# First and last batch: spectral products for f and S/2 - f stay apart, and the inverse transform sums them over five contraction tiles

## The chip, the cores and the metric

The kernel runs on one core of one Trainium2 chip. The metric is the device time of one execution in microseconds (us), lower is better; 215.07 is the median of three runs. A profiled execution is recorded beside them.

## What is computed

Per batch of 8: an attention that goes through 32 packed rows for each of 8 heads, then a gated long convolution over the sequence of S = 576.

```
p_packed = softmax(scale * p k^T) v
x        = softmax(scale * q p_packed^T) p_packed      # [8, 576, 512], heads side by side
x1, x2, x3 = split(x @ w_proj, 3)
x2_conv  = irfft(rfft(x2) * rfft(filter))              # along the sequence
out      = (x1 * x2_conv * x3) @ w_out
```

## The kernel before, in words

A batch goes through four stages. **front** loads kn, vn and qn (by GpSimd's DMA queue), transposes keys (kTp) and queries (qTp) on TensorE, forms both softmaxes (scores s1 and s2, exponentials e1 and e2 on ScalarE, values pv, sums zs, and the normalised weights a2 on GpSimd). **turn** projects (qp, copied by ScalarE to qm; `project(1, 0)` is one unit of four PSUM banks, `project(2)` one of two), transforms the attention weights along the sequence (fp, ez, fa) and transposes them (a2t). **middle** forms the spectrum in five tiles f0 to f4, multiplies it with the filter's spectrum (h3, htail) into tt and gm, and forms the gates x1 and x3 (their product w on VectorE). **back** does the inverse transform (x2), multiplies with w into y and yt, and projects out (o, os, written by the sync engine's queue). `together` interleaves the stages of neighbouring batches; batch 0's middle and back and batch 7's stand partly alone, at the two ends of the program.

The spectrum is folded. Frequencies f = 1 to 128 and S/2 - f share their cosine and sine rows up to a sign that depends on whether the time index is even or odd. In `spectrum(m)`, which runs in the order m = 0, 2, 1, 3, 4, tiles 0 and 2 belong to one half of the complex product and tiles 1 and 3 to the other: VectorE multiplies a tile with two filter rows (tt0 to tt3, 128 x 1024 in fp32), and GpSimd adds tt0 + tt2 and tt1 + tt3. After m = 3, four adds and subtractions of 128 x 512 combine those two sums into gm parts 0 and 1 (for even time columns) and 2 and 3 (for odd ones). gm part 4 is the tail tile. For batches 1 to 6 GpSimd does all four; for batches 0 and 7 VectorE does parts 0 and 1, and GpSimd 2 and 3.

`inverse(m)` then makes, for each 128 of the 512 channels, a block of 288 even and 224 odd time columns with three matmuls each (two gm parts of that parity and the tail; ac holds the three tables), and `inverse_left` the last 64 odd columns for all four channel blocks in one bank.

The order of the work on each engine is not that of the code. All operations are recorded, and a planner simulates the five engines and the DMA queues and lists the operations in the order in which it would start them: on every engine the earliest recorded operation that is ready and whose buffers are free (`fits`). PSUM has eight banks (tag "ps"), at most six for the kinds "attention" and "transform" each. A unit, such as a projection, starts only when all its banks are free at once. The planned order is fixed at build time, so an engine that waits blocks all that stands behind it in its queue. Line 344 (354 after the change) is the recorder's call and so the line of nearly every row.

Of the kernel before, what the change touches and what calls it, by code (L numbers as in the profile page):

```python
# [14 lines left out]
ALU = mybir.AluOpType  # L15
AX = mybir.AxisListType

P = 128
SC_Y = float(2.0 ** 16)
# [13 lines left out]
COLUMN_T = np.concatenate([TILE_T[1], TILE_T[3], TILE_T[4], TILE_T[2][:64], TILE_T[0], TILE_T[2][64:]])  # L33
# [4 lines left out]
def _f16(x):  # L38
    return np.asarray(x, dtype=np.float64).astype(np.float16)


def _constants(S):
    F = S // 2 + 1
    t = np.arange(S, dtype=np.float64)
    f = np.arange(F, dtype=np.float64)
    ang = 2.0 * np.pi * np.outer(f, t) / S
    wre = np.cos(ang)
    wim = -np.sin(ang)
    cf = np.full(F, 2.0)
# [12 lines left out]

    inv = np.stack([
        are[F_LO], aim[F_LO],
        np.concatenate([are[F_TAIL], are[0:1], -are[F_TAIL], are[F - 1:F],
                        aim[F_TAIL], zero, aim[F_TAIL], zero], axis=0)])


    wc = np.zeros((P, 4, 384), dtype=np.float16)
    wt = np.zeros((P, 2, 640), dtype=np.float16)  # L70
    for i in range(4):
        wc[:, i, 0:256] = _f16(low[:, TILE_T[i]].T)
        wc[:, i, 256:384] = _f16(tail[:, TILE_T[i]].T)
    wt[0:32, 0, 0:256] = _f16(low[:, TILE_T[4][0:32]].T)
    wt[32:64, 0, 256:512] = _f16(low[:, TILE_T[4][32:64]].T)
    wt[0:64, 0, 512:640] = _f16(tail[:, TILE_T[4]].T)
    wt[64:128, 1, :] = wt[0:64, 0, :]
    ac = _f16(inv[:, :, COLUMN_T].transpose(1, 0, 2))
    return wc, wt, np.ascontiguousarray(ac)


# [55 lines left out]
class Recorder:  # L137
# [62 lines left out]
    def plan(self):  # L200
# [56 lines left out]
            ops = op.unit or [op]  # L257
            return {r[0] for o in ops for r in o.writes + o.reads if r[0] in self.slot and r[0] not in opened}

        def fits(op):  # L260
            if op.unit and (op is not op.unit[0] or any(o.need != o.inner for o in op.unit)):
                return False
            more = {}
            for t in news(op):
                for tag, _ in self.slot[t]:
                    more[tag] = more.get(tag, 0) + 1
            if any(used[tag] + n > limit[tag] for tag, n in more.items()):
                return False
            return op.what != "dma_start" or op.engine != "POOL" or lanes[0] > 0

        def release(op, same):
            for o in op.then:
# [5 lines left out]
        def issue(e, t):  # L278
            while free[e] <= t + 1e-6:
                if e == "PE" and rest:  # L280
                    op = rest.pop(0)
                else:
                    op = min((o for o in ready[e] if fits(o)), key=lambda o: o.n, default=None)
                    if op is None:
                        return
                    for x in news(op):
                        opened.add(x)
                        for tag, _ in self.slot[x]:
                            used[tag] += 1
                    rest.extend((op.unit or [op])[1:])  # L290
                ready[e].remove(op)
                order.append(op)
                if op.what == "dma_start":
                    took = 760 if e == "POOL" else 60
                    if e == "POOL":
                        lanes[0] -= 1
                    at(t + took + (2000 if e == "POOL" else 1500), "start", op)
                else:
                    took, land = product(op, t) if e == "PE" else (op.ns(), op.ns() + 60)
                    at(t + land, "done", op)  # L300
                    release(op, True)
                free[e] = t + took
                at(t + took, "free", e)
# [47 lines left out]
def kernel(  # L351
# [16 lines left out]
    ND = DM // P  # L368
# [22 lines left out]
    def psm(name, shape, dtype=FP32):  # L391
        return nc.tile(ps, shape, dtype, "ps", 8, name, ("transform", 6))
# [326 lines left out]
    def middle(b):  # L719

        s = st[b]
        a2t, qm, fa = s["a2t"], s["qm"], s["fa"]
        gm = sb([P, 5, DM], FP16, tag="gm", name=f"gm_b{b}")
        w = sb([P, ND, S], FP32, tag="w", name=f"w_b{b}")
        s["gm"], s["w"] = gm, w
        tt = {}

        def spectrum(m):
            f = psm(f"f{m}_b{b}", [P, DM])
            for t in range(2):  # L730
                nc.tensor.matmul(f[:], fa[:, t, ts(m, P)], qm[:, t, ts(1, DM)], start=(t == 0), stop=(t == 1))
            if m == 4:
                nc.vector.tensor_tensor(out=gm[:, 4, :], in0=f[:], in1=htail[:], op=ALU.mult)
                return
            r = m % 2
            x = tt[m] = sb([P, 2, DM], FP32, tag=f"tt{m // 2}", name=f"tt{m // 2}_b{b}", bufs=2)
            h = h3[:, r, 1:3, :] if m == 0 or m == 3 else h3[:, r, 0:2, :]
            nc.vector.tensor_tensor(out=x[:], in0=f[:].unsqueeze(1).broadcast_to([P, 2, DM]), in1=h, op=ALU.mult)
            if m >= 2:
                nc.gpsimd.tensor_tensor(out=x[:], in0=tt[r][:], in1=x[:], op=ALU.add)  # L740
            if m == 3:
                g = [tt[2], tt[3]]
                even = nc.vector if b in (0, B - 1) else nc.gpsimd

                even.tensor_tensor(out=gm[:, 0, :], in0=g[0][:, 0, :], in1=g[1][:, 0, :], op=ALU.add)
                even.tensor_tensor(out=gm[:, 1, :], in0=g[0][:, 1, :], in1=g[1][:, 1, :], op=ALU.subtract)
                nc.gpsimd.tensor_tensor(out=gm[:, 2, :], in0=g[0][:, 0, :], in1=g[1][:, 0, :], op=ALU.subtract)
                nc.gpsimd.tensor_tensor(out=gm[:, 3, :], in0=g[0][:, 1, :], in1=g[1][:, 1, :], op=ALU.add)

        def gate(*ms):  # L750

            cols = slice(0, MAIN) if len(ms) == 1 else slice(MAIN, S)
            n = cols.stop - cols.start
            x1 = psm(f"x1_b{b}", [P, len(ms), n])
            x3 = psm(f"x3_b{b}", [P, len(ms), n])
            for x, c0 in ((x1, 0), (x3, 2 * DM)):
                for m in ms:
                    for t in range(2):
                        nc.tensor.matmul(x[:, m - ms[0], :], qm[:, t, ds(c0 + m * P, P)], a2t[:, t, cols],
                                         start=(t == 0), stop=(t == 1))  # L760
            x1s = sb([P, len(ms), n], FP32, tag="x1s", name=f"x1s_b{b}", bufs=2)
            nc.scalar.copy(out=x1s[:], in_=x1[:])
            nc.vector.tensor_tensor(out=w[:, ms[0]:ms[-1] + 1, cols], in0=x1s[:], in1=x3[:], op=ALU.mult)

        for n, m in enumerate((0, 2, 1, 3, 4)):
            spectrum(m)
            yield 1100
            if n < 4:
                gate(n)
                yield 870  # L770
        gate(*range(ND))
        yield 460
    pair = [None]

    def back(b):

# [5 lines left out]
            pair[0] = sb([P, ND, 2, 64], FP16, tag="yt", name=f"yt_b{b}", bufs=1)  # L782
        yt = pair[0]

        def inverse(m):
            x2 = psm(f"x2_b{b}", [P, MAIN])
            for e, cols in enumerate((slice(0, EVEN), slice(EVEN, MAIN))):
                for j in range(3):
                    nc.tensor.matmul(x2[:, cols], gm[:, 4 if j == 2 else 2 * e + j, ts(m, P)], ac[:, j, cols],
                                     start=(j == 0), stop=(j == 2))  # L790
            nc.vector.scalar_tensor_tensor(out=y[:, m, :], in0=w[:, m, 0:MAIN], scalar=SC_Y, in1=x2[:],
                                           op0=ALU.mult, op1=ALU.mult)

        def inverse_left():
            x2 = psm(f"x2t_b{b}", [P, ND, 64])
            for m in range(ND):
                for j in range(3):
                    nc.tensor.matmul(x2[:, m, :], gm[:, 4 if j == 2 else 2 + j, ts(m, P)], ac[:, j, MAIN:S],
                                     start=(j == 0), stop=(j == 2))
            nc.vector.scalar_tensor_tensor(out=yt[:, :, x, :], in0=w[:, :, MAIN:S], scalar=SC_Y, in1=x2[:],  # L800
                                           op0=ALU.mult, op1=ALU.mult)

        def project_out(n):

# [19 lines left out]
        for m in range(ND):  # L824
            inverse(m)
            yield 660
        inverse_left()
        yield 350
        for n in range(5 if x else 4):
            project_out(n)  # L830
# [71 lines left out]
```

## Time and profile before

| | |
|---|---|
| runs | 214.38, 215.07, 216.06 us; median 215.07 |
| profiled execution | 215.93 us, span 214.1 us from first to last instruction |
| mean granted TensorE clock | 0.953 |
| TensorE matmul busy | 187.0 us, 87% of the span |
| VectorE, ScalarE, GpSimd busy | 149.5, 127.4, 140.1 us |

Batches overlap, so these shares are means over stages with different limits. In a timeline row stand the start, the length, the engine, the operation with the tiles it writes and reads (buffer numbers left out, so x_b is any of x1, x2, x3), its shape, how often it was repeated, and in brackets the idle time before it with what ended it. A matmul's length includes its way through the array; the pace is read from the starts.

### The profile page before, as it was taken

To read this page: it belongs to the slowest core of one execution; us is meant where nothing else is said; L and a number is where in the kernel's file an instruction comes from. 1 tells how busy PE (TensorE), PEld (TensorE's weight loads), DVE (VectorE), ACT (ScalarE), POOL (GpSimd) and SP (SyncE) were. 2 spreads that over 40 slices of the span, in tenths; PEclk is the share of its full clock that TensorE was granted. 3 is DMA by queue.
4 is the path that set the end of the run, shared out by engine and by line. 5 is a ranking of instruction groups with operands and counts; after the bars stand their busy time and mean duration, and the time that the engine had idled before them with its cause. 6 is when DMAs were issued, how large, how long until landed. Compare 5 with 4: busy or idle time off the path is not lost.

```text
span 214.1 us, 5815 instructions
## 1 busy us (share of the span) xinstructions
PE 187.0 (87%) x2418; PEld 117.0 (55%) x2418; DVE 149.5 (70%) x276; ACT 127.4 (59%) x269; POOL 140.1 (65%) x112
## 2 busy tenths in 40 slices
PE   0777559994999999999999999999999999997890
PEld 0225427651866566566765676566756565653540
DVE  4243837999257959886796699477957987698530
ACT  2236567593187897785757766777687846334040
POOL 8612388659464769989966699179447995945500
PEclk9999958997699999999999999999999999999796
DMA  5999999999999999069489990043013103405016
GB/s 123 285 217 202 207 197 201 207 197 193 164 168 218 237 156 144 4 92 236 129 112 159 149 215 3 8 134 106 3 49 94 59 0 124 127 0 182 19 65 180
DMA packets 36523, 28.71 MB, mean 134 GB/s; under 512 B 8016, under 2 KB 31056, under 8 KB 36496
## 3 DMA queue, kind: packets, MB, share of 16 engines
q0 software_dynamic: 29312, 16.52, 57.0%
q1 hardware_dynamic: 6464, 11.10, 17.0%
q10 hardware_dynamic: 720, 0.72, 1.1%
q8 instruction: 19, 0.31, 0.6%
q14 instruction: 8, 0.07, 0.1%
HBM read 35.41 MB, written 9.44 MB: 209 GB/s over the span
## 4 chain that ended last, share of the span: by engine, by line
PE 65%; DVE 16%; DMA 6%; POOL 5%; issue 3%; ACT 2%; DVEq 0%; POOLq 0%
PE x_b L344 20%; PE o_b L344 13%; PE f_b L344 7%; DMA kn_b<-in_k_dram 6%; PE fp_b L344 6%; PE s_b L344 4%; DVE tt_b L344 3%; PE qTp_b L344 3%; DVE gm_b L344 3%; PE pv_b L344 2%; DVE zs_b L344 2%; PE kTp_b L344 2%; PE qp_b L344 2%; POOL gm_b L344 2%; PE a2tp_b L344 2%
## 5 line engine op out<-in xcount | busy, mean ns | idle before, releaser
L344 POOL TENSOR_TENSOR tt_b<-tt_b,tt_b 128x1024 f32<-128x1024 f32 x16 | 37.7, 2359 | 14.4 <-DVE tt_b L344 14.4
L344 DVE TENSOR_TENSOR tt_b<-f_b,h 128x1024 f32<-128x1024 f32 x32 | 38.9, 1218 | 6.4 <-PE f_b L344 4.4
L344 PE MATMUL x_b<-a2t_b,qm_b 128*128 128x512 f16 (+1 forms) x256 | 42.0, 286 | 0.4 <-DVE w_b L344 0.3
L344 POOL TENSOR_TENSOR gm_b<-tt_b,tt_b 128x512 f16<-128x512 f32 x28 | 36.6, 1337 | 0.5
L344 ACT ACTIVATE os_b<-o_b 128x512 f32<-128x512 f32 x36 | 21.5, 607 | 23.7 <-PE o_b L344 23.5
L344 PE MATMUL x_b<-ac,gm_b 128*128 128x288 f16 (+1 forms) x192 | 30.5, 295 | 5.0 <-DVE gm_b L344 4.7
L344 PE MATMUL o_b<-wout,y_b 128*128 128x512 f16 x128 | 33.6, 380 | 0.2 <-DVE y_b L344 0.2
L344 PEld LDWEIGHTS <-gm_b 128*128 128x128 f16 x288 | 22.9, 104 | 15.0 <-DVE gm_b L344 5.7
L344 ACT CAST qm_b<-qp_b 128x512 f16<-128x512 f32 x48 | 25.1, 609 | 4.7 <-PE qp_b L344 4.4
L344 POOL TENSOR_TENSOR fa_b<-ez_b 128x512 f16<-128x512 f32 x14 | 17.5, 1269 | 14.7 <-ACT ez_b L344 14.7
L344 ACT COPY x1s_b<-x_b 128x512 f32<-128x512 f32 (+1 forms) x40 | 22.3, 560 | 8.2 <-PE x_b L344 8.0
L344 DVE TENSOR_TENSOR w_b<-x1s_b,x_b 128x512 f32<-128x512 f32 (+1 forms) x40 | 24.9, 625 | 1.6 <-ACT x1s_b L344 1.4
L344 ACT ACTIVATE e_b<-s_b 96x384 f16<-96x384 f32 (+1 forms) x48 | 23.5, 532 | 3.8 <-PE s_b L344 3.7
L344 PE MATMUL f_b<-qm_b,fa_b 128*128 128x512 f16 x80 | 24.0, 380 | 0.0
L344 PEld LDWEIGHTS <-a_b 128*128 128x128 f16 x240 | 17.1, 101 | 11.6 <-POOL a_b L344 2.8
L344 DVE SCALAR_TENSOR_TENSOR y_b<-w_b,x_b 128x512 f16<-128x512 f32 x32 | 20.3, 678 | 3.2 <-PE x_b L344 3.1
L344 PEld LDWEIGHTS <-qm_b 128*128 128x128 f16 x256 | 15.9, 98 | 8.9 <-issue 1.6
L344 PEld LDWEIGHTS <-y_b 128*128 128x128 f16 x128 | 12.1, 98 | 12.2 <-DVE y_b L344 1.1
L344 POOL TENSOR_TENSOR a_b<-e_b,zr_b 128x1152 f16<-128x1152 f16 (+2 forms) x10 | 17.3, 1742 | 0.7 <-DVE zr_b L344 0.5
L344 ACT COPY ez_b<-fp_b 128x512 f32<-128x512 f32 x16 | 9.8, 610 | 12.2 <-PE fp_b L344 12.2
L344 PE MATMUL kTp_b<-ident,kn_b 96*128 96x96 f16 x192 | 12.4, 206 | 1.0 <-DMA kn_b<-in_k_dram 0.8
L344 PEld LDWEIGHTS <-kn_b 96*128 96x128 f16 x192 | 10.5, 97 | 3.9 <-DMA kn_b<-in_k_dram 1.3
(78 smaller groups left out, 300.6 us busy)
## 6 DMA issues: line engine op xcount, KB each, us to landing
out_dram<-os_b SPq DMA_DIRECT2D x24, 256.0 KB, 2.6
kn_b<-in_k_dram POOLq DMA_DIRECT2D x8, 576.0 KB, 11.4
vn_b<-in_v_dram POOLq DMA_DIRECT2D x8, 576.0 KB, 12.7
qn_b<-in_q_dram POOLq DMA_DIRECT2D x8, 512.0 KB, 9.1
out_dram<-os_b SPq DMA_DIRECT2D x16, 128.0 KB, 2.4
wp<-in_moe_w_proj_dram POOLq DMA_DIRECT2D x3, 512.0 KB, 20.7
filt<-in_moe_filter_fft_dram SPq DMA_DIRECT2D x4, 256.0 KB, 6.5
out_dram<-os_b SPq DMA_DIRECT2D x16, 64.0 KB, 2.1
```

The lines of the kernel that those rows point to most:

```text
L344: ins = op.call(*op.args, **op.kw).ins
```

## The change

For batches 0 and 7 (`APART`) the four combining adds after m = 3 are gone. GpSimd's two adds, in fp32 as before on their way in, write gm parts 0 and 1 (products for f, ready after m = 2) and 2 and 3 (products for S/2 - f, after m = 3) directly in fp16. The inverse transform of these batches sums five contraction tiles: parts 0 and 1 over all 512 columns in one matmul each, parts 2 and 3 with tables that differ between even and odd columns, so that each takes two matmuls (288 and 224 columns), and the tail over all 512. The last 64 columns take five matmuls per channel block in place of three. The table ac grows from three parts to four (576 KB in place of 432). For batches 1 to 6 the arithmetic is as it was, but all four combining operations stay on GpSimd as before.

The planner also changes for all batches: when a unit is ready and finds too few free banks, the banks that it wants are held back, so that no later recorded operation may open a new one ahead of it (`held`, `choose`).

```diff
-    ac = _f16(inv[:, :, COLUMN_T].transpose(1, 0, 2))
+    inv = inv[:, :, COLUMN_T]
+    ac = _f16(np.stack([*inv, np.where(COLUMN_T % 2 == 0, -inv[1], -inv[0])]).transpose(1, 0, 2))
...
-            if any(used[tag] + n > limit[tag] for tag, n in more.items()):
+            if any(used[tag] + held.get(tag, 0) + n > limit[tag] for tag, n in more.items()):
+                if op.unit:
+                    for tag, n in more.items():
+                        held[tag] = max(held.get(tag, 0), n)
                 return False
...
+        def choose(e):
+            held = {}
+            return next((o for o in sorted(ready[e], key=lambda o: o.n) if fits(o, held)), None)
...
-            if m >= 2:
+            if apart and m >= 2:
+                nc.gpsimd.tensor_tensor(out=gm[:, 2 * r:2 * r + 2, :], in0=tt[r][:], in1=x[:], op=ALU.add)
+            elif m >= 2:
                 nc.gpsimd.tensor_tensor(out=x[:], in0=tt[r][:], in1=x[:], op=ALU.add)
-            if m == 3:
+            if m == 3 and not apart:
                 g = [tt[2], tt[3]]
-                even = nc.vector if b in (0, B - 1) else nc.gpsimd
...
+        def terms(x2, m, cols):
+            both = slice(cols.start, min(cols.stop, EVEN)), slice(max(cols.start, EVEN), cols.stop)
+            if b in APART:
+                yield x2, gm[:, 0, ts(m, P)], ac[:, 0, cols]
+                yield x2, gm[:, 1, ts(m, P)], ac[:, 1, cols]
+                for j in (0, 1):
+                    for e, c in enumerate(both):
+                        if c.start < c.stop:
+                            yield (x2[:, c.start - cols.start:c.stop - cols.start], gm[:, 2 + j, ts(m, P)],
+                                   ac[:, j if e == j else 3, c])
+                yield x2, gm[:, 4, ts(m, P)], ac[:, 2, cols]
```

Three places show how the order of instructions moves. The first is TensorE at the start of batch 0's inverse transform. Before, it stood behind both projection units of batch 1 (qp) and all key transposes of batch 2, and its first matmul was one for 288 columns:

```order
L344 LDWEIGHTS ppk1_77
L344 MATMUL qp_b1_213<-wp_68,ppk1_77 32x512
L344 LDWEIGHTS ppk1_77
L344 MATMUL qp_b1_214<-wp_68,ppk1_77 32x512
L344 LDWEIGHTS gm_b0_162
L344 MATMUL x2_b0_209<-ac_67,gm_b0_162 128x288
L344 LDWEIGHTS gm_b0_162
L344 MATMUL x2_b0_220<-ac_67,gm_b0_162 128x288
```

Now two matmuls for 512 columns follow the last gate matmul (x3) of batch 0 at once, and the unit of four projection banks comes behind them:

```order
L354 MATMUL x3_b0_202<-a2t_b0_141,qm_b0_133 128x64
L354 LDWEIGHTS gm_b0_162
L354 MATMUL x2_b0_209<-ac_67,gm_b0_162 128x512
L354 LDWEIGHTS gm_b0_162
L354 MATMUL x2_b0_209<-ac_67,gm_b0_162 128x512
L354 LDWEIGHTS ppk1_77
L354 MATMUL qp_b1_211<-wp_68,ppk1_77 32x512
```

Behind that unit (16 matmuls) stand 12 key transposes, one more 512-column pass, and only then the first matmul with part 2. The other projection unit, the other 12 key transposes and 12 scores are now spread among the rest of the inverse.

The second place is GpSimd's queue around the two adds of batch 0 (tt or gm written from tt0 and tt1; a2 is batch 1's normalisation). Before:

```order
L344 TENSOR_TENSOR tt1_b0_174<-tt0_b0_165,tt1_b0_174 128x1024
L344 DMA kn_b3_204<-in_k_dram 96x8x384
L344 DMA vn_b3_205<-in_v_dram 96x8x384
L344 TENSOR_TENSOR tt1_b0_196<-tt0_b0_189,tt1_b0_196 128x1024
L344 TENSOR_TENSOR a2_b1_184<-e2_b1_183,zr_b1_186 128x1152
L344 TENSOR_TENSOR gm_b0_162<-tt1_b0_174,tt1_b0_196 128x512 x2
L344 DMA qn_b3_206<-in_q_dram 128x8x256
```

After:

```order
L354 DMA kn_b3_204<-in_k_dram 96x8x384
L354 TENSOR_TENSOR gm_b0_162<-tt0_b0_165,tt1_b0_174 128x1024
L354 DMA vn_b3_205<-in_v_dram 96x8x384
L354 DMA qn_b3_206<-in_q_dram 128x8x256
L354 TENSOR_TENSOR gm_b0_162<-tt0_b0_189,tt1_b0_196 128x1024
L354 TENSOR_TENSOR a2_b1_184<-e2_b1_183,zr_b1_186 128x1152
```

The issue of kn moved ahead of the first add and that of qn ahead of the second; the two combining adds are gone.

The third place is TensorE at the end, behind the last gate matmul of batch 7. Before, the first matmuls of all four channel blocks need a combined part:

```order
L344 MATMUL x3_b7_764<-a2t_b7_693,qm_b7_674 128x64
L344 LDWEIGHTS gm_b7_728
L344 MATMUL x2_b7_767<-ac_67,gm_b7_728 128x288
L344 LDWEIGHTS gm_b7_728
L344 MATMUL x2_b7_768<-ac_67,gm_b7_728 128x288
L344 LDWEIGHTS gm_b7_728
L344 MATMUL x2_b7_769<-ac_67,gm_b7_728 128x288
```

Now six passes over 512 columns, with parts 0 and 1 for three channel blocks, stand ahead of the first that needs part 2 or 3; here the last of the six and what follows:

```order
L354 MATMUL x2_b7_769<-ac_67,gm_b7_728 128x512
L354 LDWEIGHTS gm_b7_728
L354 MATMUL x2_b7_769<-ac_67,gm_b7_728 128x512
L354 LDWEIGHTS gm_b7_728
L354 MATMUL x2_b7_767<-ac_67,gm_b7_728 128x288
L354 LDWEIGHTS gm_b7_728
L354 MATMUL x2_b7_767<-ac_67,gm_b7_728 128x224
```

TensorE has 24 matmuls more in all, 12 for each of the two batches. In batches 1 to 6 the four-bank unit of `project(1, 0)` now comes ahead of `project(2)` and of some key transposes and gates, with its four casts on ScalarE; before it came behind them.

More of the change, by code (lines that the diff above doesn't have):

```diff
@@ L258, in news, with fits @@
             return {r[0] for o in ops for r in o.writes + o.reads if r[0] in self.slot and r[0] not in opened}
-        def fits(op):
+        def fits(op, held):
             if op.unit and (op is not op.unit[0] or any(o.need != o.inner for o in op.unit)):
@@ L282, in issue @@
                 else:
-                    op = min((o for o in ready[e] if fits(o)), key=lambda o: o.n, default=None)
+                    op = choose(e)
                     if op is None:
@@ L725, in middle @@
         s["gm"], s["w"] = gm, w
-        tt = {}
+        tt, apart = {}, b in APART
         def spectrum(m):
@@ L738, in spectrum @@
             nc.vector.tensor_tensor(out=x[:], in0=f[:].unsqueeze(1).broadcast_to([P, 2, DM]), in1=h, op=ALU.mult)
-            if m >= 2:
+            if apart and m >= 2:
+                nc.gpsimd.tensor_tensor(out=gm[:, 2 * r:2 * r + 2, :], in0=tt[r][:], in1=x[:], op=ALU.add)
+            elif m >= 2:
                 nc.gpsimd.tensor_tensor(out=x[:], in0=tt[r][:], in1=x[:], op=ALU.add)
-            if m == 3:
+            if m == 3 and not apart:
                 g = [tt[2], tt[3]]
-                even = nc.vector if b in (0, B - 1) else nc.gpsimd
[L745 to L748, printed above, removed]
+                for n, r, op in ((0, 0, ALU.add), (1, 1, ALU.subtract), (2, 0, ALU.subtract), (3, 1, ALU.add)):
+                    nc.gpsimd.tensor_tensor(out=gm[:, n, :], in0=g[0][:, r, :], in1=g[1][:, r, :], op=op)
         def gate(*ms):
@@ L772, in middle @@
         yield 460
-    pair = [None]
+    pair, APART = [None], (0, B - 1)
     def back(b):
@@ L783, in back @@
         yt = pair[0]
[L785 to L801, printed above, removed]
+        def terms(x2, m, cols):
[9 more added lines that the diff above has]
+                yield x2, gm[:, 4, ts(m, P)], ac[:, 2, cols]
+            else:
+                for e, c in enumerate(both):
+                    for j in range(3) if c.start < c.stop else ():
+                        yield (x2[:, c.start - cols.start:c.stop - cols.start],
+                               gm[:, 4 if j == 2 else 2 * e + j, ts(m, P)], ac[:, j, c])
@@ new lines, in inverse @@
+        def inverse(*ms):
+            cols = slice(0, MAIN) if len(ms) == 1 else slice(MAIN, S)
+            n = cols.stop - cols.start
+            x2 = psm(f"x2_b{b}", [P, len(ms), n])
+            for m in ms:
+                todo = list(terms(x2[:, m - ms[0], :], m, cols))
+                for i, (to, lhs, rhs) in enumerate(todo):
+                    first = i == 0 if b in APART or len(ms) > 1 else i in (0, 3)
+                    last = i == len(todo) - 1 if b in APART or len(ms) > 1 else i in (2, 5)
+                    nc.tensor.matmul(to, lhs, rhs, start=first, stop=last)
+            to = y[:, ms[0], :] if len(ms) == 1 else yt[:, :, x, :]
+            nc.vector.scalar_tensor_tensor(out=to, in0=w[:, ms[0], cols] if len(ms) == 1 else w[:, :, cols], scalar=SC_Y,
+                                           in1=x2[:, 0, :] if len(ms) == 1 else x2[:], op0=ALU.mult, op1=ALU.mult)
@@ L826, in back @@
             yield 660
-        inverse_left()
+        inverse(*range(ND))
         yield 350
```

## The prediction

> **What bounds the kernel now.** First the page's engine shares and the stretches of the windows view (columns: stretch, length, busy time of PE, PEld, DVE, ACT and POOL with instruction counts, then the granted TensorE clock, DMA share, GB/s).
>
> ```profile
> PE 187.0 (87%) x2418; PEld 117.0 (55%) x2418; DVE 149.5 (70%) x276; ACT 127.4 (59%) x269; POOL 140.1 (65%) x112
> ...
> 50.00:55.00 5.00, 3.56 (x14) 1.89 (x15) 3.08 (x5) 0.00 (x0) 5.00 (x5) 0.55 1.31 196
> 55.00:60.00 5.00, 4.86 (x59) 4.11 (x58) 2.30 (x5) 1.29 (x4) 0.79 (x2) 0.77 1.21 158
> ...
> 155.00:165.00 10.00, 10.00 (x160) 5.99 (x156) 6.42 (x13) 7.91 (x17) 5.42 (x4) 1.00 0.18 65
> ...
> 196.80:204.00 7.20, 5.09 (x41) 3.76 (x38) 4.77 (x7) 0.28 (x1) 4.08 (x3) 0.77 0.20 58
> ```
>
> TensorE is the bound over most of the span: 155 to 165 us is full of matmuls at full clock, while every other engine rests at times. Two stretches are not like that, and both are where batch 0 and batch 7, the two that the change touches, form their products: around 50 us TensorE is partly idle at a clock of 0.55, and from 196.8 us it works 5.09 of 7.20 us at 0.77. In the timeline of TensorE (start, length, operation) and of VectorE and GpSimd beside it, the first looks like this:
>
> ```profile
> 44.81 0.91 PE L344 MATMUL qp_b<-wp,ppk 64*32 64x512 f16 x8
> 45.65 1.19 PE L344 MATMUL kTp_b<-ident,kn_b 96*128 96x96 f16 x24
> 47.98 0.41 PE L344 MATMUL qp_b<-wp,ppk 64*32 64x512 f16 x7 [0.17 <-ACT kT L344]
> 50.40 0.63 PE L344 MATMUL x_b<-ac,gm_b 128*128 128x288 f16 x2 [2.01 <-DVE gm_b L344]
> 52.07 2.58 PE L344 MATMUL x_b<-ac,gm_b 128*128 128x288 f16 x10 [1.04 <-DVE gm_b L344]
> ...
> 58.49 0.56 PE L344 MATMUL qTp_b<-ident,qn_b 128*128 128x128 f16 x7
> 58.94 0.39 PE L344 MATMUL o_b<-wout,y_b 128*128 128x512 f16 x1
> 59.19 0.35 PE L344 MATMUL s_b<-pk,kT 128*128 128x64 f16 x6
> 59.38 0.22 PE L344 MATMUL qTp_b<-ident,qn_b 128*128 128x128 f16 x1
> ...
> 62.67 0.44 PE L344 MATMUL pv_b<-ones,e_b 96*128 96x1 f16 x12
> ```
> ```profile
> 47.99 4.03 DVE L344 TENSOR_TENSOR gm_b<-tt_b,tt_b 128x512 f16<-128x512 f32 x2
> ...
> 45.34 2.35 POOL L344 TENSOR_TENSOR tt_b<-tt_b,tt_b 128x1024 f32<-128x1024 f32 x1 [2.23 <-DVE tt_b L344]
> 47.67 2.13 POOL L344 TENSOR_TENSOR a_b<-e_b,zr_b 128x1152 f16<-128x1152 f16 x1
> ```
>
> GpSimd's second add has waited for VectorE's product with spectrum tile 3 until 45.34 and ends at 47.69, and then VectorE takes 4.03 us for two combining adds, 2.0 each, beside a busy GpSimd. TensorE, which meets the inverse next in its fixed order, waits 2.01 + 1.04 us, and the clock falls: (1 - 0.55) and (1 - 0.77) of 5 us, doubled, are 6.8 us at half speed. The end shows the same chain:
>
> ```profile
> 196.28 0.63 PE L344 MATMUL x_b<-a2t_b,qm_b 128*128 128x64 f16 x16
> 198.21 0.66 PE L344 MATMUL x_b<-ac,gm_b 128*128 128x288 f16 x4 [1.30 <-DVE gm_b L344]
> 199.34 0.20 PE L344 MATMUL x2t_b<-ac,gm_b 128*128 128x64 f16 x1 [0.47 <-POOL gm_b L344]
> 199.88 3.64 PE L344 MATMUL x_b<-ac,gm_b 128*128 128x288 f16 x20 [0.35 <-DVE gm_b L344]
> 203.32 0.79 PE L344 MATMUL x2t_b<-ac,gm_b 128*128 128x64 f16 x11
> 203.92 3.68 PE L344 MATMUL o_b<-wout,y_b 128*128 128x512 f16 x16
> ...
> 188.89 2.35 POOL L344 TENSOR_TENSOR tt_b<-tt_b,tt_b 128x1024 f32<-128x1024 f32 x1 [1.34 <-DVE tt_b L344]
> 195.07 2.36 POOL L344 TENSOR_TENSOR tt_b<-tt_b,tt_b 128x1024 f32<-128x1024 f32 x1 [3.82 <-DVE tt_b L344]
> ...
> 202.26 2.48 DVE L344 SCALAR_TENSOR_TENSOR y_b<-w_b,x_b 128x512 f16<-128x512 f32 x4 [2.43 <-PE x_b L344]
> ```
>
> **Rates at full clock.** From the start of one group to the start of the next:
>
> ```profile
> 173.54 0.51 PE L344 MATMUL x2t_b<-ac,gm_b 128*128 128x64 f16 x12
> 173.89 0.60 PE L344 MATMUL f_b<-qm_b,fa_b 128*128 128x512 f16 x2
> 174.32 0.38 PE L344 MATMUL fp_b<-wt,a_b 128*128 128x512 f16 x1
> 174.54 0.60 PE L344 MATMUL fp_b<-wc,a_b 128*128 128x256 f16 x4
> 174.98 0.81 PE L344 MATMUL o_b<-wout,y_b 128*128 128x512 f16 x3
> ```
>
> 512 columns take 0.43 / 2 = 0.215 us, 64 columns 0.35 / 12 = 0.029, one fp bank 0.66. A main block of the inverse is three passes of 512 columns before (0.645 us) and five after (1.075, the split pairs counted by their columns). The last block has 20 matmuls instead of 12. **Added TensorE work** for one batch: 4 x 0.43 + 8 x 0.029 = 1.95 us, 3.9 us for both.
>
> A 64-column matmul also loads 128 weight columns of its own. The Trainium skill, TensorE: Matmul & The Clock Gate, section "LDWEIGHTS (loading the stationary operand)", gives columns / 1.2 ns, an estimate of 107 ns for each load; if that set the pace, the eight more would cost 0.86 us a batch instead of 0.23 and the forecast would rise by 1.3 us. The trace disagrees: 12 of them started within 0.35 us.
>
> **The last batch.** Products for f (gm 0 and 1) now come straight from the first GpSimd add, which ended at 191.24. TensorE is done with the gate's sixteen 64-column matmuls at 196.28 + 16 x 0.029 = 196.74 and can go on with six 512-column passes until 198.03. The second add ends at 197.43, so nothing waits. The inverse takes 4 x 1.075 + 20 x 0.029 = 4.88 us, to 201.62. The output projection, at 203.92 now, begins **2.3 us earlier**. Its fourth operand needs the last of the y products: the last main block ends near 201.05, one product is 2.48 / 4 = 0.62, so 201.85, before the fourth matmul at 202.27. I take 2.2; the bounds are 1.5 (each y a full 0.62 late) and 2.4. Two VectorE adds and two GpSimd adds vanish there; at this end nobody is queued behind them.
>
> **The start.** The table ac grows from three to four parts, and it travels ahead of most of the first key load:
>
> ```profile
> GB/s 123 285 217 202 207 197 201 207 197 193 164 168 218 237 156 144 4 92 236 129 112 159 149 215 3 8 134 106 3 49 94 59 0 124 127 0 182 19 65 180
> ac<-c_ac SPq DMA_DIRECT2D x1, 432.0 KB, 7.7
> 16.63 0.94 PE L344 MATMUL kTp_b<-ident,kn_b 96*128 96x96 f16 x18 [0.84 <-DMA kn_b<-in_k_dram]
> ```
>
> 144 KB more at 217 GB/s (third slice) are 0.68 us, and TensorE waited for that key load. Bounds 0 and 0.7; I take **0.65 late**, because the transfers run without a pause from there to past 40 us, and the later loads slip with it.
>
> **The first batch.** The gate ended at 44.81; now 45.45. TensorE does two 512-column passes (0.43), the unit of 16 projections (twice the first row's eight at most), 12 key transposes (half of 1.12, from 45.65 to 46.77) and one more pass, 1.8 to 2.9 us, and then waits for the second add: 47.69 + 0.65 = **48.35**, up to 1.1 us. From there to the values product at 62.67 it has left: inverse 4 x 1.075 + 0.58 - 0.645 = 4.24; 12 key transposes 0.56; 8 projections 0.84; 24 scores at 0.19 for six, 0.77; 17 query and p transposes at 0.45 for seven, 1.09; two fp banks 1.32; 8 output matmuls 1.72. That is 10.5. To it I add 0.5 for one new wait:
>
> ```profile
> 47.79 2.10 ACT L344 CAST qm_b<-qp_b 128x512 f16<-128x512 f32 x4
> ```
>
> ScalarE's second copy of pk now stands behind two casts, 2 x 0.53, and the scores wait for it; behind it on ScalarE are the exponentials for batch 2 (bounds 0 and 1.1). 48.35 + 10.5 + 0.5 + 0.2 for mode switches gives 59.6: **3.1 earlier** than 62.67, the 0.65 included. With no wait for pk and none for the switches 3.8; with the clock lost again, see below, nothing or less.
>
> **Batches 1 to 6** keep their arithmetic. The planner's new reservation pulls the four-bank projection unit ahead of key transposes and gates on TensorE, and its four casts ahead on ScalarE. I cost this at nothing: TensorE is full there and its work the same. Between 60 and 196 us the waits view has TensorE waiting for ScalarE for 0.7 us, of which this row is the most:
>
> ```profile
> PE s_b L344 <- ACT kT L344: 0.5, 1, 0.5
> ```
>
> Bounds: one such wait more, or fewer, in every second batch, 1.5 us either way.
>
> **Sum**, against the profiled run of 215.93 us (span 214.1 and 1.8 around it): 3.1 + 2.2 = 5.3 less, 210.6. That run lay 0.86 above the median of 215.07, so the forecast is **209.8**.
>
> **The rivals.**
> *The clock still falls in batch 0.* The end shows that it falls after waits of 1.30 + 0.47 + 0.35 us; a wait of 1.1 among short key transposes is half of that. Price: up to 6.8 us at half speed again, 3.4, giving 213.2. The Trainium skill, TensorE: Matmul & The Clock Gate, section "Why this matters for your kernels", allows idle gaps of up to about 3 us; by that rule this rival had no chance and the sum stayed. The end's windows row (0.77 with no single gap over 1.30) speaks against the rule, so I keep it.
> *The second add is late.* GpSimd now issues the loads vn and qn of batch 3 between its two adds. Its timeline shows an issue that waited for the landing of an older load, and the issue of batch 2's kn; the third row is the key loads' own:
>
> ```profile
> 19.46 0.79 POOL L344 DMA_DIRECT2D kn_b<-in_k_dram  x1 [1.98 <-DMA vn_b<-in_v_dram]
> ...
> 30.76 0.84 POOL L344 DMA_DIRECT2D kn_b<-in_k_dram  x1
> ...
> DMA to landing us min/median/max: 6.2/11.4/13.9
> ```
>
> The load waited for was the eighth issue before it. The eighth before qn is batch 2's kn, which lands at 30.76 + 13.9 + 0.65 = 45.3 at the latest; the issue of 0.9 then ends near 46.2, just when the add's input is there (45.34 + 0.65 = 46.0). One landing later (576 KB at 200 GB/s, 2.9 us) gives 212.7, with the clock lost 216.
> *The planner's new order is better in the steady part*: 2 us, 207.8.
> *Slower.* The four-bank unit stands in TensorE's fixed order and blocks all behind it until four evictions are done. Four casts of 0.53 a batch waited out in full, six times, are 12.7 us: 222. It decides from (5.3 + 2.15) / 6 = 1.24 us a batch. The waits view's 0.7 us for the whole stretch speaks against it.
>
> **How the numbers follow.** Forecast 0.58; better steady order 0.12; clock 0.12; late add 0.08; slower 0.10. One per cent, 2.15 us, is about what a measurement of this kernel can tell from no change. Faster by more (under 212.9): forecast, better order and about a third of the clock and late cases, 0.76; within it 0.15; slower by more 0.09. The range runs from 206.8 (better order, kind ends of the terms) to 213.8 (clock lost).
>
> **What would show it.** No row of VectorE combining adds; at the end x_b starting right behind the gate without a gap, and the output matmuls about 7.2 us after the gate's end no more, but 4.9; in the windows a clock of 1.00 from 45 to 60 and over the end; pv of batch 2 near 59.6; kTp's first start near 17.3. It is wrong if TensorE's idle time in the steady part grows, or if its wait before batch 0's inverse is over 1.5 us.

## The result, and the profile after

The changed kernel takes **207.94 us** (median of four runs, 207.40 to 208.14), the kernel before 214.72 (213.74 to 216.06; the three runs of before and one more): ratio 0.9676, 95% interval 0.9618 to 0.9734, 6.8 us less. The forecast was 209.8, 5.3 us less. Profiled, the execution took 207.86 us, span 206.1. Ratios, here and below, leave out runs more than 1.5% above the fastest of the same kernel (among them the profiled one of the products apart without the holding, 472.49 us, so that none of its rows are shown).

From the page (engine shares, then the granted TensorE clock in 40 slices) and the windows view of the changed kernel, over the stretches that were shown of before (at the end 5.25 us earlier, from the gate's end on) and the one from 45 to 50:

```profile
PE 185.6 (90%) x2442; PEld 116.4 (56%) x2442; DVE 144.3 (70%) x272; ACT 128.2 (62%) x269; POOL 133.6 (65%) x108
...
PEclk9999658999999999999999999999999999999997
```
```profile
45.00:50.00 5.00, 4.54 (x52) 2.74 (x52) 4.84 (x9) 3.03 (x7) 4.97 (x3) 1.00 1.66 188
50.00:55.00 5.00, 5.00 (x80) 3.60 (x78) 2.87 (x7) 3.85 (x9) 2.79 (x4) 1.00 1.33 203
55.00:60.00 5.00, 5.00 (x108) 3.64 (x107) 1.01 (x5) 3.52 (x7) 2.98 (x3) 1.00 1.92 177
155.00:165.00 10.00, 10.00 (x170) 6.30 (x168) 7.85 (x15) 7.03 (x17) 9.07 (x7) 1.00 0.27 82
191.55:198.75 7.20, 7.20 (x65) 4.38 (x62) 3.81 (x7) 1.24 (x3) 0.68 (x1) 1.00 0.20 58
```

TensorE's idle stretches at both ends are nearly gone: 50 to 55 us is full (3.56 of 5.00 before), the end is full (5.09 of 7.20 before), and the clock is 1.00 in both. In the middle TensorE is full, as it was. Low digits are left in the clock row in slices 5 to 7, ahead of batch 0's gate, and in the last, behind the last matmul. The row of before has them there too, and also in slices 10 and 11, the first batch, and 38, the end:

```profile
PEclk9999958997699999999999999999999999999796
```

TensorE's timeline of the changed kernel shows how the first batch and the end now run, and, in the first row, where batch 0's key load, the first of all, is waited for:

```profile
14.91 0.94 PE L354 MATMUL kTp_b<-ident,kn_b 96*128 96x96 f16 x18 [0.69 <-DMA kn_b<-in_k_dram]
...
43.88 0.63 PE L354 MATMUL x_b<-a2t_b,qm_b 128*128 128x64 f16 x16
44.56 0.59 PE L354 MATMUL x_b<-ac,gm_b 128*128 128x512 f16 x2
45.08 0.81 PE L354 MATMUL qp_b<-wp,ppk 64*32 64x512 f16 x16
45.82 0.79 PE L354 MATMUL kTp_b<-ident,kn_b 96*128 96x96 f16 x12
46.68 0.38 PE L354 MATMUL x_b<-ac,gm_b 128*128 128x512 f16 x1
47.44 1.69 PE L354 MATMUL x_b<-ac,gm_b 128*128 128x288 f16 x11 [0.39 <-POOL gm_b L354]
...
50.46 0.41 PE L354 MATMUL qp_b<-wp,ppk 64*32 64x512 f16 x8
50.81 0.82 PE L354 MATMUL x_b<-ac,gm_b 128*128 128x512 f16 x4
...
57.40 0.44 PE L354 MATMUL pv_b<-ones,e_b 96*128 96x1 f16 x12
...
191.08 0.63 PE L354 MATMUL x_b<-a2t_b,qm_b 128*128 128x64 f16 x16
191.55 5.08 PE L354 MATMUL x_b<-ac,gm_b 128*128 128x512 f16 x48
196.47 3.62 PE L354 MATMUL o_b<-wout,y_b 128*128 128x512 f16 x16
```
```profile
43.82 0.89 POOL L354 DMA_DIRECT2D qn_b<-in_q_dram  x1 [1.48 <-PE f_b L354]
45.03 2.35 POOL L354 TENSOR_TENSOR gm_b<-tt_b,tt_b 128x1024 f16<-128x1024 f32 x1 [0.33 <-DVE tt_b L354]
```

At 47.44 the inverse meets GpSimd's second add, which ended at 45.03 + 2.35 = 47.38, after a wait of 0.39 us in place of 2.01 + 1.04. Two passes, sixteen projections, twelve key transposes and one more pass (from 44.56 on) cover most of that add. At the end 48 matmuls of the inverse follow the gate with no wait at all.

The span splits at four marks that both kernels have: the start of batch 0's last gate matmuls, x3 from a2t (43.88; before it is the row below), the values product of batch 2 (62.67, 57.40), the start of batch 7's last gate group (196.28, 191.08) and the output projection at the end (203.92, 196.47).

```profile
44.14 0.63 PE L344 MATMUL x_b<-a2t_b,qm_b 128*128 128x64 f16 x16
```

| stretch | before | after | difference | forecast |
|---|---|---|---|---|
| start to batch 0's gate | 44.14 | 43.88 | -0.26 | +0.65 |
| gate to values product (first batch) | 18.53 | 13.52 | **-5.01** | -3.7 |
| to batch 7's gate (steady) | 133.61 | 133.68 | +0.07 | 0 |
| gate to output projection (end) | 7.64 | 5.39 | **-2.25** | -2.2 |
| output projection to the end | 10.18 | 9.63 | -0.55 | 0 |
| span | 214.1 | 206.1 | -8.0 | -5.3 |

(The forecast for the first batch is 3.1 and the 0.65 lost at the start.) The two profiled executions differ by 8.1 us, the medians by 6.8, since that of before lay 1.2 over its median.

### The profile page after: what moved, and what is told of

The parts are those of the page before. It is cut to its first block, busy times and chain, and to the rows that moved or that the text cites. A ratio compares the mean times of both kernels' runs of the same rounds, so it can differ in the third digit from the quotient of the medians.

```text
span 206.1 us, 5861 instructions
## 1 busy us (share of the span) xinstructions
PE 185.6 (90%) x2442; PEld 116.4 (56%) x2442; DVE 144.3 (70%) x272; ACT 128.2 (62%) x269; POOL 133.6 (65%) x108
## 4 chain that ended last, share of the span: by engine, by line
PE 58%; POOL 17%; DMA 11%; DVE 6%; ACT 4%; issue 2%; POOLq 0%; ACTq 0%; DVEq 0%
PE x_b L354 20%; PE o_b L354 11%; DMA wp<-in_moe_w_proj_dram 11%; POOL gm_b L354 8%; PE fp_b L354 6%; PE f_b L354 5%; POOL tt_b L354 5%; PE s_b L354 4%; DVE tt_b L354 3%; PE qTp_b L354 3%; PE pv_b L354 3%; ACT qm_b L354 2%; PE qp_b L354 2%; PE kTp_b L354 2%; POOL fa_b L354 1%
## 5 line engine op out<-in xcount | busy, mean ns | idle before, releaser
L354 POOL TENSOR_TENSOR gm_b<-tt_b,tt_b 128x512 f16<-128x512 f32 (+1 forms) x28 | 39.2, 1427 | 6.0 <-DVE tt_b L354 5.5
L354 PE MATMUL x_b<-a2t_b,qm_b 128*128 128x512 f16 (+1 forms) x256 | 40.5, 286 | 0.0
L354 PE MATMUL x_b<-ac,gm_b 128*128 128x64 f16 (+3 forms) x312 | 35.7, 253 | 1.1 <-POOL gm_b L354 0.8
L354 PE MATMUL o_b<-wout,y_b 128*128 128x512 f16 x128 | 32.9, 379 | 0.2 <-DVE y_b L354 0.2
L354 POOL TENSOR_TENSOR tt_b<-tt_b,tt_b 128x1024 f32<-128x1024 f32 x12 | 28.3, 2356 | 5.9 <-DVE tt_b L354 5.9
L354 PEld LDWEIGHTS <-gm_b 128*128 128x128 f16 x312 | 22.2, 98 | 9.9 <-POOL gm_b L354 3.4
L354 ACT ACTIVATE e_b<-s_b 96x384 f16<-96x384 f32 (+1 forms) x48 | 24.3, 530 | 2.4 <-PE s_b L354 2.1
L354 DVE SCALAR_TENSOR_TENSOR y_b<-w_b,x_b 128x512 f16<-128x512 f32 x32 | 20.9, 679 | 3.0 <-PE x_b L354 2.8
L354 PE MATMUL kTp_b<-ident,kn_b 96*128 96x96 f16 x192 | 13.4, 206 | 0.7 <-DMA kn_b<-in_k_dram 0.7
L354 POOL DMA_DIRECT2D qn_b<-in_q_dram x8 | 7.2, 896 | 9.4 <-PE qTp_b L354 4.8
```

The costliest lines, as they stand in the source:

```text
L354: ins = op.call(*op.args, **op.kw).ins
```

## The experiments

Theory: the time comes from the waits for the combining adds at the two ends, and from the half-speed clock that these waits bring on; the planner's holding of banks and the wider table are worth nothing or cost a little. Rivals: the gain is the planner's; it is all in one of the ends; the clock has no part in it.

**The holding alone**, on the kernel before:

```diff
+ held[tag] = max(held.get(tag, 0), n)      # in fits; choose(e) picks by it
```

> The kernel before, with the planner's holding back of banks for a waiting unit and nothing else of the change. Theory (the gain comes from the two places where batch 0 and batch 7 form their products, the order of the steady part is worth nothing): no change within 1 per cent, 212.6 to 216.9 us against 214.7; TensorE still waits about 3 us for VectorE's combining adds ahead of batch 0's inverse and 2 us at the end, and the granted clock falls at both. Rival (the planner's order is what gains): 208 to 210 us.

Measured: 215.23, ratio 1.0009 (0.9974 to 1.0044): no change. Its TensorE timeline still has the waits for the combining adds, 2.12 and 0.77 us in the first batch:

```profile
49.41 0.90 PE L351 MATMUL x_b<-ac,gm_b 128*128 128x288 f16 x3 [2.12 <-DVE gm_b L351]
51.08 2.34 PE L351 MATMUL x_b<-ac,gm_b 128*128 128x288 f16 x9 [0.77 <-DVE gm_b L351]
...
198.26 0.20 PE L351 MATMUL x2t_b<-ac,gm_b 128*128 128x64 f16 x1 [0.46 <-POOL gm_b L351]
198.81 3.79 PE L351 MATMUL x_b<-ac,gm_b 128*128 128x288 f16 x20 [0.35 <-DVE gm_b L351]
```
```profile
50.00:55.00 5.00, 4.23 (x19) 2.55 (x18) 2.08 (x4) 0.00 (x0) 4.69 (x5) 0.50 1.27 192
199.00:203.00 4.00, 4.00 (x32) 3.19 (x31) 1.68 (x3) 0.00 (x0) 0.88 (x1) 0.57 0.02 4
```

The windows rows behind it show the clock: 0.50 in the first batch, 0.57 at the end.

**The products apart, without the holding:**

```diff
-                if op.unit:
-                    for tag, n in more.items():
-                        held[tag] = max(held.get(tag, 0), n)
```

> The change without the planner's holding back of banks. Theory: 207 to 209.5 us, nearly all of the 6.8 us that the whole change gained, with the clock at full from 34 us to the end of the matmuls; in batch 0 six to eight 512-column passes stand ahead of the first that needs the second add, so its wait of 0.39 us may go, at most 0.4 us faster. Rival (the planner's order is what gains): 213 to 215 us.

Measured: ratio 0.9664 (0.9625 to 0.9704), beside the change's 0.9676. Within these intervals the whole gain is in the products kept apart, and none shows that is the order rule's.

**One end at a time**, VectorE and GpSimd combining in the other batch as before:

```diff
-    pair, APART = [None], (0, B - 1)
+    pair, APART = [None], (B - 1,)          # last only;  (0,) for first only
```

> The change with the products kept apart for batch 7 alone; batch 0 combines as before, with VectorE on parts 0 and 1. Theory: the end gains its 2.26 us and batch 0 nothing: 212 to 213 us; the clock still falls around 50 us. Rival (the gain at batch 0 comes from the moved units and transposes, not from the adds): 208 to 210 us.

> The change with the products kept apart for batch 0 alone; batch 7 combines as before, with VectorE on parts 0 and 1. Theory: batch 0's gain without the end's, 4.5 us: 209.5 to 211 us; the clock stays at full from 34 us to about 195 us and falls at the end again; from the gate's end to the output projection at the end about 7.2 us. Rival as for the kernel with batch 7 alone: the same 208 to 210 us there, and here no more than there.

Measured: last only 212.32, ratio 0.9859 (0.9808 to 0.9911); first only 210.51, ratio 0.9781 (0.9728 to 0.9834). The two gains, 1.4 and 2.2%, add to 3.6%, within their intervals the 3.2% of the change. By stretches they are also separate. Last only has 18.21 us from gate to values product (before 18.53), at half clock by its windows row, and 200.47 - 195.08 = 5.39 at the end (5.39 in the changed kernel):

```profile
50.00:55.00 5.00, 3.08 (x14) 1.96 (x15) 3.53 (x5) 0.00 (x0) 4.62 (x6) 0.50 1.33 202
```
```profile
195.08 0.63 PE L354 MATMUL x_b<-a2t_b,qm_b 128*128 128x64 f16 x16
195.55 5.08 PE L354 MATMUL x_b<-ac,gm_b 128*128 128x512 f16 x48
200.47 3.62 PE L354 MATMUL o_b<-wout,y_b 128*128 128x512 f16 x16
```

First only has 13.68 in the first batch, and at the end the old waits, but not the low clock that was expected of them (timeline, then the windows row of that stretch):

```profile
190.76 0.63 PE L354 MATMUL x_b<-a2t_b,qm_b 128*128 128x64 f16 x16
192.69 0.67 PE L354 MATMUL x_b<-ac,gm_b 128*128 128x288 f16 x4 [1.30 <-DVE gm_b L354]
193.81 0.20 PE L354 MATMUL x_b<-ac,gm_b 128*128 128x64 f16 x1 [0.46 <-POOL gm_b L354]
194.36 2.62 PE L354 MATMUL x_b<-ac,gm_b 128*128 128x288 f16 x31 [0.35 <-DVE gm_b L354]
196.82 3.75 PE L354 MATMUL o_b<-wout,y_b 128*128 128x512 f16 x16
```
```profile
190.76:197.50 6.74, 4.63 (x56) 3.39 (x55) 4.81 (x7) 0.74 (x2) 4.59 (x3) 1.00 0.24 70
```

Waits of 1.30 + 0.46 + 0.35, those of before to 0.01 us, and a clock of 1.00. So gate to output projection is 196.82 - 190.76 = 6.06 there, against 7.64 with the clock lost and 5.39 with the products apart. The kernel of the next experiment, with the same waits and the clock kept there as well, has 6.07. Of the 2.25 us won at the end of the profiled run, 1.6 are the clock and 0.7 the waits less the added matmuls.

**The clock by itself.** The kernel before, its combining adds untouched, with 12 matmuls whose result nothing reads put in front of batch 0's inverse, where TensorE waits anyway (the planner orders what follows anew):

```diff
+        if b == 0:
+            keep = psm("keep", [P, DM])
+            for _ in range(WARM):       # WARM = 12
+                nc.tensor.matmul(keep[:], ident[:], gm[:, 4, :], start=True, stop=True)
```

> The kernel before with twelve additional matmuls of 512 columns, whose result nobody reads, on TensorE between the last projection of batch 1 and batch 0's inverse, where it waits for VectorE's combining adds; they need the tail product (gm part 4), so they start near 48 us and end near 51. The wait for the adds stays. Theory (the half clock after the wait costs as much as the wait itself, 6.8 us at half speed less the 1.0 us of it that was idle, halved: 2.9 us): the clock does not fall around 50 us, 212 to 213 us against 214.9. Rival (only the wait counts, the slower matmuls are hidden behind VectorE and ScalarE): 214.5 to 215.5 us with the clock at full.

Measured: 212.52, ratio 0.9906 (0.9870 to 0.9941). TensorE's timeline and windows, the last two rows of each from the end:

```profile
46.32 0.91 PE L345 MATMUL qp_b<-wp,ppk 64*32 64x512 f16 x8
...
49.84 2.76 PE L345 MATMUL keep<-gm_b,ident 128*128 128x512 f16 x12
53.60 0.76 PE L345 MATMUL x_b<-ac,gm_b 128*128 128x288 f16 x5 [0.88 <-DVE gm_b L345]
...
61.28 0.44 PE L345 MATMUL pv_b<-ones,e_b 96*128 96x1 f16 x12
...
196.82 0.66 PE L345 MATMUL x_b<-ac,gm_b 128*128 128x288 f16 x4 [1.30 <-DVE gm_b L345]
...
198.50 2.31 PE L345 MATMUL x_b<-ac,gm_b 128*128 128x288 f16 x20 [0.35 <-DVE gm_b L345]
```
```profile
50.00:55.00 5.00, 4.12 (x25) 2.11 (x24) 4.83 (x7) 1.66 (x4) 5.00 (x4) 1.00 1.29 191
55.00:60.00 5.00, 5.00 (x77) 4.12 (x76) 3.81 (x7) 2.96 (x7) 3.85 (x5) 1.00 1.02 128
...
200.00:206.00 6.00, 5.57 (x40) 2.74 (x37) 2.81 (x5) 2.41 (x5) 0.00 (x0) 1.00 0.18 67
194.00:200.00 6.00, 3.89 (x40) 2.62 (x39) 4.03 (x5) 0.98 (x3) 5.49 (x3) 1.00 0.32 92
```

The clock stays at 1.00 in the first batch, and from the projections' start to the values product it takes 14.96 us, against 62.67 - 44.81 = 17.86 before: 2.9 less with work added and none removed. The new order can have little part in it: behind the last wait, from 52.07 to 62.67, TensorE idles for 0.23 us in the kernel before. The profile of before gives the price a second way: behind that wait the clock is at half until 57.3, 5.2 us, and half of that is 2.6. Keeping the clock up is thus worth 2.6 to 2.9 of the 5.0 us of the first batch; the rest are the shorter waits (2.01 + 1.04 less 0.39) and what else the new order brings, less the longer inverse; these were not taken apart.

That the whole time came out as expected is in part luck. In the profiled executions (213.00 and 215.93 us) the first batch won 2.9, counted from the gate, the gate came 1.5 later (45.65), and the end won 1.6: there too the clock stayed at 1.00, after the same waits as before. How much of the difference of the medians is the first batch alone is not known.

**The wider table alone**: the kernel before, with the four-part table loaded, and with four parts in memory of which three are loaded.

```diff
+    ac = _f16(np.stack([*inv, np.where(COLUMN_T % 2 == 0, -inv[1], -inv[0])]).transpose(1, 0, 2))    # both kernels
...
+        if far.size() == P * 4 * 576 and far.shape[-1] == 576:    # four loaded: the planner prices three
+            return P * 3 * max(1152 / 24.6, 22) / 16
...
-    nc.sync.dma_start(ac[:], d_ac.ap()[:])
+    nc.sync.dma_start(ac[:], d_ac.ap()[:, 0:NI, :])               # three of four loaded: NI = 3
```

> The kernel before with the table of four parts loaded (576 KB in place of 432 KB), the fourth part unused, and every engine's order as before. Theory of the prediction (144 KB more ahead of the first key load): the load lands 0.65 us later than in the kernel before, near 16.9 us, and the time is 0.3 per cent longer at most. Rival (what the traces of three kernels with four parts show, first key load at 14.6 to 15.1 us, though pages with three parts have 16.2 and 16.6): the wider table itself makes the first loads land sooner, near 14.9, and the time is 0 to 1.3 us shorter.

> The kernel before with the table of four parts lying in memory and only three of them loaded (432 KB), every engine's order as before. If the table's transfer makes the first loads sooner, the first key load lands as before, 16.2 to 16.6 us. If it is where the constants lie in memory, it lands near 14.3 us, and the time is up to 2 us shorter. If it is neither, as with the three parts.

Measured: loaded 215.57, ratio 1.0043 (1.0007 to 1.0079); stored only 214.73, ratio 0.9995 (0.9952 to 1.0039). On the key load the rival of the first kernel was right (near 14.9 expected) and so was the first theory of the second (16.2 to 16.6): it is the wider transfer that brings the load forward, not the place of the constants. Neither kernel got faster for it. The first row is that of the kernel with four parts loaded, the second that with three of four (from an execution of 217.70 us):

```profile
14.76 0.94 PE L347 MATMUL kTp_b<-ident,kn_b 96*128 96x96 f16 x18 [0.64 <-DMA kn_b<-in_k_dram]
```
```profile
16.55 1.18 PE L345 MATMUL kTp_b<-ident,kn_b 96*128 96x96 f16 x18 [1.62 <-DMA kn_b<-in_k_dram]
```

With 144 KB more ahead of it, the key load lands 1.9 us sooner than before (14.76 against 16.63), and the time is 0.9 us longer all the same, or 0.15 by the lower end of the interval; over all runs of both the medians are 215.57 and 215.20, only 0.4 apart. The order of instructions was held the same. What it lost again is not settled. Its profiled execution, the shortest of its twelve (214.04), can't tell. The mean clock of the twelve was 0.940, that of the 23 runs behind the ratio 0.953, and over those 23 a clock lower by 0.01 went with 0.7 us more: 0.9 us for the 0.013. That is a correlation, not a test.

**All batches apart:**

```diff
-    pair, APART = [None], (0, B - 1)
+    pair, APART = [None], tuple(range(B))
```

> The change with the products kept apart for all eight batches: 72 matmuls more on TensorE than in the changed kernel, 24 combining operations fewer on GpSimd. Theory (between the two ends TensorE sets the pace and each batch pays its added 1.95 us in full): 6 x 1.95 = 11.7 us more than the changed kernel's 207.9, 218 to 220 us, and the stretch from the values product of batch 2 to the last gate of batch 7 grows from 133.7 to about 145.4 us. Rival (the steady part waits for GpSimd's combining as the ends did, and the matmuls hide behind it): 206 to 210 us.

Measured: 218.42, ratio 1.0178 (1.0109 to 1.0248). The timeline has the values product at 58.08 and batch 7's gate at 201.82:

```profile
58.08 0.44 PE L354 MATMUL pv_b<-ones,e_b 96*128 96x1 f16 x12
...
201.82 0.63 PE L354 MATMUL x_b<-a2t_b,qm_b 128*128 128x64 f16 x16
```
```profile
155.00:165.00 10.00, 10.00 (x157) 6.63 (x155) 6.18 (x10) 6.37 (x12) 4.47 (x3) 1.00 0.13 49
```

The steady stretch is 143.74 us, 10.1 more than the change's, or **1.68 us a batch** (1.95 was worked out). GpSimd is busy for 69.3 us of that stretch in place of 98.6, and it buys nothing: TensorE waits for it there for 0.4 us in all in the changed kernel, and is busy 131.9 of 133.7 us. The same edit pays at the ends and costs in the middle.

**The table later**, behind the first two batches' loads on GpSimd's queue:

```diff
-    nc.sync.dma_start(ac[:], d_ac.ap()[:])
     load(1)
+    nc.gpsimd.dma_start(ac[:], d_ac.ap()[:])          # wout's load moved behind load(2)
```

> The changed kernel with its table of four parts moved from the sync queue, where it goes beside the first key load, to GpSimd's queue behind batch 1's loads, and the output weights moved behind batch 2's. Theory (the start is bound by the transfers ahead of the first key load): that load lands about 2.6 us sooner, near 12.3 us (576 KB at 217 GB/s), and the time falls by 1 to 2.5 us, to 205.5 to 207. Rival (the start is bound by the filter's loads and the chain behind them, or the later loads come late instead): 207.5 to 209 us.

Measured: 205.80 (205.21 to 206.29), ratio 0.9586 (0.9542 to 0.9630). TensorE's first key transpose is at 13.73, not the 12.3 expected, batch 0's gate at 42.26 and the values product of batch 2 at 55.46:

```profile
13.73 0.43 PE L354 MATMUL kTp_b<-ident,kn_b 96*128 96x96 f16 x6 [0.76 <-DMA kn_b<-in_k_dram]
...
42.26 0.63 PE L354 MATMUL x_b<-a2t_b,qm_b 128*128 128x64 f16 x16
...
55.46 0.44 PE L354 MATMUL pv_b<-ones,e_b 96*128 96x1 f16 x12
```

Of 1.94 us at the values product 1.62 were there at batch 0's gate already (42.26 against 43.88). So the start does set the end here. The intervals of the two ratios just touch, but no run of this kernel is as long as the shortest of the change's (206.29 and 207.40).

**The table later and no holding:**

> The changed kernel with its table on GpSimd's queue behind batch 1's loads, and without the planner's holding back of banks, so that eight 512-column passes stand ahead of the first matmul of batch 0 that needs the second add. Theory: TensorE's wait for the second add there goes, at most 0.4 us: 205.2 to 206 us, no difference from the 205.8 with the late table alone that can be told. Rival (the projection units, now later, hold up batch 1's casts and its spectrum): 206.5 to 208 us.

Measured: 205.01 (204.41 to 205.79), ratio 0.9565 (0.9519 to 0.9611). The wait for the second add was expected to go. This order has one of 0.50 us, while TensorE has none for it with the holding, by the waits view of the kernel with the late table from 42 to 56 us:

```profile
45.77 2.13 PE L351 MATMUL x_b<-ac,gm_b 128*128 128x288 f16 x15 [0.50 <-POOL gm_b L351]
```

It is the fastest version run, 9.3 us under the kernel before and 2.4 under the change by the ratios. Against the late table with holding it is not told apart: the intervals overlap.

## Why the prediction was right, and where it was off

**What bounds the kernel** held: TensorE in the middle, the chain of GpSimd's second add and the combining adds at the ends. The last-only and first-only kernels show both ends, each by itself.

**The end** held: 2.2 forecast, 2.25 measured. The gate's end to the output projection is 196.47 - 191.55 = 4.92 us against 4.9. The inverse's 48 matmuls, 20 of them of 64 columns, fill it at the paces of the rates part. The Trainium skill's price for a weight load (TensorE: Matmul & The Clock Gate, section "LDWEIGHTS (loading the stationary operand)") would, by an estimate, have made it some 0.6 us longer for the eight added loads; that is not seen here either. The composition was not foreseen: 1.6 of it hung on the clock, which was not lost there in every profiled execution with these waits, so that the agreement of the size is in part luck. (One sum on the way is off without consequence: 201.05 and 0.62 are 201.67, not 201.85; both are ahead of 202.27.)

**The first batch** was mis-sized: 3.7 forecast from the gate on, 5.0 measured. The step that failed is the list of work from the second add to the values product, 10.5 + 0.5 + 0.2 = 11.2 us; it took 57.40 - 47.44 = 9.96. The eight projections were priced at 0.84 from one row of before and took 50.81 - 50.46 = 0.35 (in the steady part of before, from 75.08 on, sixteen take 0.56); the 0.5 for a new wait for pk did not come, since TensorE is busy 5.00 of 5.00 us in both stretches from 50 to 60; these are 1.0 of the 1.2, and the 0.2 set aside for mode switches was not needed either. The second add itself was met as forecast, 2.9 us behind the gate's end then, 2.8 now (47.38 - 44.56), with a shorter wait: 0.39 where up to 1.1 was allowed.

**The start** failed in sign: +0.65 forecast for the wider table, and the key load came 1.7 us sooner (14.91 against 16.63) with the gate 0.26 us sooner. The four-part table did that to the key load alone, on the old kernel too. What became of it at the gate this pair can't show: over the traces with three parts loaded the gate starts at 43.14 to 47.10 us, over those with four at 43.10 to 43.95, and the half-speed piece on the way differs, with a mean clock from 22 to 38 us of 0.79 in the kernel before and 0.68 in the changed one. The step "144 KB more at 217 GB/s" took one queue's bytes as time for another's landing, and these transfers went the other way.

**Batches 1 to 6** at nothing: +0.07 us in the trace, and the holding alone 1.0009.

**The added TensorE work**, 1.95 us a batch, was 1.68 by the kernel with all batches apart; what made it less was not looked into.

**The rivals.** The clock did not fall in batch 0: 1.00 from 45 us on. The price of losing it, "3.4", was near: 2.6 to 2.9. In the kernel with the holding alone no gap at the two ends was over 2.12 us and the clock fell at both; gaps of 1.30, 0.46 and 0.35 us at the end had it in the kernel before, and not in first only and with the idle matmuls. The Trainium skill's rule on idle gaps of about 3 us (same page, "Why this matters for your kernels") does not agree with these rows. The add was not late because of the issue of qn: that ended at 43.82 + 0.89 = 44.71, and the add then waited 0.33 for VectorE. The planner's order was neither better nor worse (1.0009 alone), and nothing shows the four-bank unit holding anybody up: TensorE's waits in the steady stretch are 1.4 us in all, and 1.5 before.

Summed up, the profiled execution gained 8.1 us where 5.3 were forecast: 1.3 more in the first batch, 0.9 at the start, 0.55 behind the start of the last projection, up to where the output lands. That 0.55, put at nothing, goes with batch 7's products: this stretch is 9.57 to 9.63 us in the five traces with them apart and 10.08 to 10.28 in the six without. All the misses go the same way, so none hid another. The medians differ by 6.8 alone, since that of before (214.72) lies 1.2 under its profiled run; 0.86 had been set off.

## What to carry to other kernels

Ask of every engine that looks overloaded who waits for it, and where: giving TensorE 1.7 us a batch more, to take adds off GpSimd and VectorE, won 2.3 us at the end and 5 at the first batch, and lost in every batch between. A wait of two or three us on TensorE is to be priced with the low clock that can follow it, here up to about as much again as the wait, and filling the wait with matmuls that nothing reads shows that part, if it is read from the stretch and not from the whole time. A rate for a sum is to be read from more than one row of the same shape.

## What the runs showed of the hardware that was not expected

- The same three waits (1.30, 0.46 to 0.47, 0.34 to 0.35 us) at the end were followed by half speed in the kernel before, with the holding alone and with the wider table loaded, and not in first only and with the idle matmuls. What decides is not settled. It is not the length of the waits alone, nor how far into the run they come: the gate ahead of them starts at 194.61 (wider table loaded) and 195.20 us (holding alone) where the clock fell, and at 194.89 (idle matmuls) where it stayed.
- Half speed lasted some 3.4 us or a multiple of it (from the windows view: twice the missing clock, times the stretch). At the end it was 3.2 to 3.5 us, in the first batch 6.7 to 7.0, but 3.5 in both kernels of the wider-table experiment, and ahead of batch 0's gate about 7, 10, 14 or 21, with no edit that explains it: 7 in the kernel before and 10 in the one with the idle matmuls, whose code up to there is the same. Traces of single executions differ by that.
- A load of 576 KB in place of 432 KB on one queue let the first key load on another land 1.7 to 1.9 us sooner (14.91 and 14.76 against 16.63). With the fourth part stored but not loaded it was 16.55. Over all traces with the table on that queue it is 14.76 to 15.25 us with four parts loaded (five kernels) and 16.24 to 17.03 with three (four). The cause was not found.
- Taking that table off the early queue altogether brought the key load to 13.73 only.
